# Talking-heads attention, then a SoLU MoE layer, on one core: another stored order for the attention steps

## The chip, the core and the metric

The kernel runs on one core of a Trainium2 chip. Five engines work at once, each through its own list of instructions in order: TensorE (PE, with its weight loads PEld) multiplies, VectorE (DVE) and ScalarE (ACT) do elementwise work and reductions, GpSimd (POOL) does elementwise work on SBUF and issues DMAs, SyncE (SP) issues DMAs. They wait for each other by semaphores. The metric is the time of one execution on the device in microseconds; three runs are given by their median.

## The reference

Attention with four batches, 12 heads, 448 positions and head size 64; the heads are mixed before and after the softmax. Its result is the input of a layer of 1792 tokens.

```python
scores = scale * np.matmul(q, k.transpose(0, 1, 3, 2))
scores = np.einsum('bhij,hg->bgij', scores, w_pre)
attn = np.exp(scores - np.max(scores, axis=-1, keepdims=True))
attn = attn / (np.sum(attn, axis=-1, keepdims=True) + 1e-09)
x = np.matmul(np.einsum('bhij,hg->bgij', attn, w_post), v)   # then (1792, 768)
h = x @ w_in                                                  # (1792, 1024)
solu = h * softmax(h)
out = (layer_norm(solu) * g_ln) @ w_out                       # (1792, 768)
```

## The kernel before

Matrices are split into a high and a low 16-bit part, and a product is the sum of three products of parts. The high part is a scaled copy (line 394 on ScalarE, 396 on GpSimd). The low part is what remains (line 399 on VectorE, lines 616 and 617 as two steps on GpSimd).

**Attention.** Per batch, q and k are loaded as raw_q and raw_k (line 558), their maximum is taken (588 to 590), and six pairs of heads each are split (pair_hi 607, pair_lo 613) into hl_q and hl_k. Here VectorE reads two SBUF tiles, the raw one and the high part. SP's DMA transposes (629) turn them into q and k. Rows are taken in four blocks per batch. For a block TensorE makes scores ps (735), ScalarE and VectorE split them into s (394, 758), and SP fetches s, rearranged, into sr (791): ten rows of all 12 heads are one unit, and units go in pairs. For a pair TensorE does the premix pm (822), VectorE the row maximum (834), ScalarE the exponential e with its sum sm (850). A guard adds a small number to sm (861, on GpSimd or VectorE), VectorE takes the reciprocal (865), GpSimd scales the postmix weights wq by it into wr (871), one step for each unit. TensorE then multiplies e by wr into o (881), which ScalarE or VectorE copies into p_t (403, 405). After a block TensorE multiplies by v into px (942), and xsh and xsl are split from it (394, 399). There are 92 pairs or single last units, and so 92 reciprocals; 180 units, and so 180 wr.

**w_in.** Before attention ends, w_in is loaded as 64-bit numbers in six pieces, each in four DMAs (cv_wi, line 1010), and made 32-bit numbers: on VectorE the exponent (1025), the sign (1031), the mantissa's mask (1036) and the join (1041), on ScalarE a rebias (1028), on GpSimd the product (1044). Its maximum follows (wm, 1066 or 1068), and a split into wi (394, 396, 399). The first MoE tile's matmuls (ps_h, 1111; tile 0 in 18 steps of two matmuls) are mixed into the end of attention.

**MoE.** For each of 14 tiles of 128 tokens: ps_h by TensorE (1111), then on VectorE, ScalarE and GpSimd the SoLU and the norm (u, line 1735 on), stores and transposes through memory, then the output product s (1937). w_out is converted in the same time, on VectorE above all; the matmul spread_wo (365) belongs to its scale.

**What sets the order.** Every step is a task with the engines that may do it. The class Plan once made an order by a model of costs; now two strings hold it, ORDER for attention and ORDER_MOE. A number is the place of the next task among those left, sorted by due time, and a letter (a, d, p, s) puts it on another engine than the first it names:

```python
for x in (order or self.ORDER).split():
    n = x.rstrip("adps")
    run, on = self.tasks[rest.pop(int(n))][:2]
    out.append(({"a": "act", "d": "dve", "p": "pool", "s": "sp"}[x[-1]] if n != x else next(iter(on)), run))
```

The steps are then issued in that order, so the string decides each engine's list. Semaphores are set by what a step reads, writes and takes over in buffers. No semaphore keeps steps apart that share no data.

Of the kernel before, what the change touches and what calls it, by code (L numbers as in the profile page):

```python
# [18 lines left out]
class Plan:  # L19
# [21 lines left out]
        "97 102 98 99 2604 2593 2596 95 2579 2582 99 95 2586 98 2574 99 93 2568 2596 2582 117 2568 2583 2573 101 100 "  # L41
        "119d 118 103 110a 95 103 119d 117 124 123d 130d 97d 121 88 88d 121d 92a 92a 89 88a 102 88a 88a 114 89 112 100d "
        "110 111 120 122d 89a 112 101 110 98 109a 89a 88 102 89 88d 105 88 88 94 92a 92d 101a 98 88 91 91 95a 102 154 "
        "88 106 94a 90 88 107 101a 103d 112 89 146 91 118 88 112p 90 88 147 115d 149 119 116a 121 152 110 100 109 116p "
        "119p 101 2497 124 101 137 146 2474 123 150 132 2490 2472 115d 2490 103 130 148 2492 116p 112p 135 2471 147 147 "
        "147 2469 93 102 2476 115a 116d 2480 95 2473 88 95 133 97 98 2469 123 127 126 104 125 0 103 118 97 104 2451 "
        "2449 120 124 102 97 97 97 2453 99p 2442 112 2439 100 2443 2438 87 121 96 98 87 113 98 112d 0 104 2437 97 110 "
        "2434 2424 115 116 86 94p 115 2427 93 2420 2418 95 96 2412 105 2413 122 86 104 86 112 95 99 120 112p 0 101 94 "
        "85 93 85 85 102 105 97 97 98a 85 91 109 91 97 98 91 85 89 89 89 111 2380 99 2382 0 88 2379 102 88 88a 2374 88 "
        "89 88 104 84d 87 106 87 91 84a 107 93p 91 86 87 91 86 89 98 96 93 92 87d 92 98 104 88 91 92 94 96d 90 96 101 "  # L50
        "87a 91 93 95 96 89 96 92 97 89d 92 96 85a 92 97 93 88d 94 84d 84 94 85a 91 97 91 96 0 85 87a 83 89p 89 92 94 "
        "95 94 93 85 2305 133 2302 97 84 87 86 83a 103 89 84a 93 94 86 0 92 92 120 94 96 93 2283 117 2280 84 96 84d 84 "
        "2276 2276 86 86 94 90 84a 97 84 97 90d 90 90 90 106 106 91 92 84 87 95 83a 84a 95 0 89 82 89 94 83a 92 95p 95 "
        "100 102 86 96 84 99 86a 87 82 0 83 94 80a 98 94 94 106 87 90 83 82 100 86 101 85 0 81 99 91 81a 104 98 99 98 "
        "83 92p 86 97 91 94 98 99 95 93 98 86 98 98 83 97 92 83d 84 94 85 96p 96 112 89 86 96 87 93 95 86 79 83a 91 80 "
        "0 90 82 89 85 95 93 107 124 101 83a 88 85 88 80 79d 88 82a 111 95 101 98 87 104 82 97 103 90d 83 0 79 109d 87 "
        "83 95 100 77p 81a 103 94 91 84 97 100 86 81 0 84 80a 104 87 103 103 85 93 87p 80 94 86 101 92 86 83d 86 77p 86 "
        "79 81a 95 81a 96 98 102 82 87 0 94 96 88d 100 82 81 82 96 104 82 84 0 79 82 74d 78a 94 82 81 87 81 78a 80 92 "
        "83 92 92 83 96 79 84d 96 98 96 96 84 99 89 90 74 78 77p 78d 79a 90 88 79 82 91 90 87d 80 80 89 99 91 90 0 84 "
        "89 94 79 90 111 81a 88 89 77p 88 81 73d 88p 103 79a 80 84 88 85 80 0 90 80 82 84 72 84 84 72d 87 78a 83 76 84 "  # L60
        "84 79 72 77 76a 78 82p 85 0 89 75 75 76 79 85 86 78 90 75a 72p 78 76 77 75 89 73d 81 73d 80 81d 88 74 0 75 73 "
        "86 70 72 76 95 77 76 72a 73a 72 76 94 70 0 70 80 78 88 69 69 70 69 74 75p 76 69 71 71 79 73 69 89 69d 69d 69 "
        "80 81p 78 71 87 87 77 70 69 70 70 69 74 0 80 70 73 72 83 68a 88 70 71 69d 71 80p 88 70 68 70 0 70 67 68a 83 73 "
        "73 93 76 73 79 76 67 0 72 66 75 89 66 67a 79 70 66 68 66 67 68 77 68 82 77 83 68 82 82 79 87 107 67a 76 69p 69 "
        "68d 102 66 85 87 67 88 68 73 77p 0 83 67 68 84 82 68a 73 85 81 65 70a 89 86 103 74 0 80 92 86 89 88 71 72 72 "
        "93 73 78p 117 85 89 89 74a 75a 67 111 75 82 88 91 73 74 90 74 84p 75 76 82 87 86 91 89 94 67 74 0 66 73a 82 95 "
        "88 90 75d 0 95 97 75 74 91 79 76 66 82d 95 74 88 96 75 80 90 76a 78a 71 79 84 78 99 87 103 79 0 92 96 100 78 "
        "84 104 100 85 80 101 94 74 81 97 94 85p 85 80a 103 93 81d 96 0 82 112 75d 79a 83 83 95 81 87 95 94 103 129 82 "
        "78 94 111 85p 91 85 122 92 96 60s 94 91 60p 79a 76 95 87a 100 80d 101 81 135 91d 82 60s 60p 74 95 79 86 79 88 "
        "90 76 123 90 95 60s 78a 88 0 97 79a 80 82 87 88p 73d 59s 86 75 95 85 59p 88 78 88 88 89 91 97 78 0 110 88 78 "  # L70
        "93 58p 117 77a 81 72 76a 98 112 76 58p 93 77 58s 77 70 96 88p 92 88 93 58s 58s 87 89 95 90 90 99 76a 92 94d 0 "
        "96 82a 92 97 58s 82 92 97 58s 96 82 98 82 58s 99 89 81a 85 97 94 87 87 97 58a 63 81a 85 85 58s 82 93p 0 92 80 "
        "91 92 81 84 92 94 95 84 80 91 80 96 92 64 96 87 80a 82a 89 0 97 82 55d 72 100 90p 91 90 63 98 93 80 93 81 96 "
# [2186 lines left out]
```

## Time and profile before

| | |
|---|---|
| time, median of 3 runs | 632.03 us (628.05 to 632.23) |
| the profiled execution | 632.41 us, span 630.7 us |
| PE busy | 600.8 us (95% of the span) |
| DVE busy | 551.4 us (87%) |
| ACT busy | 447.9 us (71%) |
| POOL busy | 324.1 us (51%) |
| attention's last work on TensorE | about 420 us after the start |

The profile is one execution. A share is a mean over both halves; matmuls are pipelined and their ends are modelled, so a busy TensorE isn't one at its peak. A wait is put down to the instruction whose semaphore came last.

### The profile page before, as it was taken

Reading aid. Unit: us, or ns where it says so; the run is one execution under the profiler, and the core shown is the slowest. Engines: PE = TensorE matmul, PEld = TensorE weight load, DVE = VectorE, ACT = ScalarE, POOL = GpSimd, SP = SyncE. Lnnn points to the kernel's source line nnn. Section 1 sums busy time; section 2 is a strip of 40 time slices with the busy share of each in tenths; the row PEclk is TensorE's granted clock in tenths of the full one; section 3 lists DMA queues with packets and bytes.
Section 4 is the critical chain, followed back from the end, with each engine's and each line's share of the span. In section 5 each row is a group of like instructions: output and inputs, shape, how many; then the busy total and the mean of one; then the engine's idle time right before and its main releaser. Section 6 shows DMA issues by size and latency. Waiting matters only on the chain. (4 is left out here: it accounts for less than half of the span.)

```text
span 630.7 us, 19859 instructions
## 1 busy us (share of the span) xinstructions
PE 600.8 (95%) x7650; PEld 405.1 (64%) x7650; DVE 551.4 (87%) x1301; ACT 447.9 (71%) x1003; POOL 324.1 (51%) x505
## 2 busy tenths in 40 slices
PE   7998999999999999998999998999997999999997
PEld 6665777777677777686777677764442445666664
DVE  5888999889999989996999998757999899997783
ACT  3688887889878788876899996625776987453320
POOL 2554586255793345971456436602536565475740
PEclk9999999999999999998999999999997999999999
DMA  7577478469887459799658855232584506069642
GB/s 176 157 158 224 154 160 207 152 202 207 227 203 194 169 192 200 230 188 228 230 165 202 260 196 212 113 85 81 180 221 119 162 35 164 20 151 202 157 117 75
DMA packets 134646, 106.80 MB, mean 169 GB/s; under 512 B 88388, under 2 KB 122600, under 8 KB 134552
## 3 DMA queue, kind: packets, MB, share of 16 engines
q1 hardware_dynamic: 128072, 91.43, 53.9%
q0 software_dynamic: 3904, 10.04, 6.4%
q10 hardware_dynamic: 2576, 4.06, 2.5%
q8 instruction: 60, 0.98, 0.7%
q14 instruction: 34, 0.28, 0.1%
HBM read 34.03 MB, written 16.97 MB: 81 GB/s over the span
## 5 line engine op out<-in xcount | busy, mean ns | idle before, releaser
L881 PE MATMUL o<-wr,e 128*64 128x120 f32 x2520 | 157.6, 271 | 5.1 <-POOL wr L871 3.4
L881 PEld LDWEIGHTS o<-wr,e 128*64 128x64 f32 x2520 | 134.8, 138 | 36.7 <-issue 19.3
L850 ACT ACTIVATE e<-pm,nb 128x448 f32<-128x448 f32 x180 | 114.4, 641 | 22.4 <-PE o L881 6.9
L834 DVE TENSOR_SCALAR_CACHE_REDUCE pm<-pm,c_nexp 128x448 f32<-128x448 f32 x171 | 113.7, 683 | 16.0 <-PE pm L822 13.9
L871 POOL TENSOR_SCALAR wr<-wq,sm 128x120 f32<-128x120 f32 x180 | 73.8, 418 | 89.7 <-DVE sm L865 66.1
L758 DVE SCALAR_TENSOR_TENSOR s<-ps,s 120x448 f16<-120x448 f32 (+1 forms) x180 | 105.1, 613 | 7.9 <-ACT s L394 6.9
L394 ACT ACTIVATE s<-ps 120x448 f16<-120x448 f32 (+1 forms) x180 | 90.7, 550 | 25.2 <-PE ps L735 20.6
L403 ACT COPY p_t<-o 128x480 f32<-128x480 f32 x148 | 89.1, 624 | 11.3 <-PE o L881 11.0
L942 PE MATMUL px<-p_t,raw_v 128*64 128x120 f32 (+3 forms) x1632 | 93.4, 258 | 0.9 <-DVE xsl L399 0.9
L1111 PE MATMUL ps_h<-wi,xf 128*128 128x512 f16 x396 | 88.4, 387 | 0.0
L942 PEld LDWEIGHTS px<-p_t,raw_v 128*64 128x64 f32 x1632 | 82.1, 137 | 7.2 <-issue 4.8
L735 PE MATMUL ps<-k,q 64*64 64x448 f16 (+2 forms) x972 | 76.7, 354 | 2.5 <-DVE q L399 0.8
L1111 PEld LDWEIGHTS <-xf 128*128 128x128 f16 x396 | 39.5, 100 | 48.5 <-issue 3.3
L822 PE MATMUL pm<-sr,wp_hi 64*64 64x448 f16 (+1 forms) x684 | 57.3, 358 | 7.2 <-DMA sr<-s 5.4
L861 POOL TENSOR_SCALAR sm<-sm 128x2 f32<-128x2 f32 (+1 forms) x59 | 15.0, 254 | 68.3 <-ACT e L850 62.3
L735 PEld LDWEIGHTS <-q 64*64 64x64 f16 (+1 forms) x972 | 32.5, 105 | 27.4 <-issue 14.7
L1937 PEld LDWEIGHTS <-sz 128*128 128x128 f16 x336 | 32.9, 98 | 21.7
L850 ACT ACTIVATION_READ_ACCUMULATOR e<-pm,nb 128x1 f32 x180 | 37.7, 209 | 0.0
L822 PE MATMUL pm<-sr,wp_lo 60*64 60x448 f16 (+1 forms) x342 | 36.6, 349 | 0.0
L1879 POOL TENSOR_TENSOR xs<-xs 128x512 f32<-128x512 f32 x14 | 24.1, 1720 | 22.2 <-DVE xs L1879 21.7
L1937 PEld LDWEIGHTS <-lt 128*128 128x128 f16 x252 | 24.7, 98 | 16.4
L822 PEld LDWEIGHTS <-wp_hi 64*64 64x64 f16 (+1 forms) x684 | 18.6, 105 | 25.6 <-issue 19.7
(250 smaller groups left out, 1111.1 us busy)
## 6 DMA issues: line engine op xcount, KB each, us to landing
sr<-s SPq DMA_DIRECT2D x176, 210.0 KB
cv_wi<-in_moe_w_in_dram SPq DMA_DIRECT2D x24, 256.0 KB
cv_wo<-in_moe_w_out_dram SPq DMA_DIRECT2D x8, 768.0 KB
raw_k<-in_k_dram POOLq DMA_DIRECT2D x18, 224.0 KB, 4.1
raw_q<-in_q_dram POOLq DMA_DIRECT2D x18, 224.0 KB, 7.7
ln_h<-lh SPq DMA_DIRECT2D x14, 256.0 KB
ln_l<-ll SPq DMA_DIRECT2D x14, 256.0 KB
xl<-xsl SPq DMA_DIRECT2D x9, 224.0 KB
```

The source lines that it names most:

```text
L394: nc.scalar.activation(out=hi, in_=x, func=AF.Copy, scale=s)
L403: nc.scalar.copy(out=out, in_=in_)
L735: nc.tensor.matmul(sps[b, c, h + e][lo:hi], q2[b, g][rows, 2 * j + x, i0 + lo : i0 + hi], k1[b, g][rows, 2 * j + y, 0:S], start=(a == 0), ...
L758: nc.vector.scalar_tensor_tensor(out=t[:, h, 1], in0=y, scalar=2.0**-E_S, in1=t[:, h, 0], op0=ALU.mult, op1=ALU.subtract)
L822: nc.tensor.matmul(pmx[b, u + i][64 * e : 64 * e + 64, 0:S], w[rows], sr[b, u][rows, e, z], start=(a == 0), stop=(a == 2),)
L834: nc.vector.tensor_scalar(out=pmx[b, u][:, 0:S], in0=pmx[b, u][:, 0:S], scalar1=c, scalar2=None, op0=ALU.mult, op1=ALU.min, accum_out=nb,)
L850: nc.scalar.activation(out=ee[b, u], in_=pmx.pop((b, u))[:, 0:S], func=AF.Exp, bias=nbs.pop((b, u)), scale=-1.0, accum_out=sm,)
L871: ENG[eng].tensor_scalar(out=w, in0=wq[0:UK, 0 : H * UN], scalar1=sm, scalar2=1.0, op0=ALU.mult, op1=ALU.mult)
L881: nc.tensor.matmul(o_t[g][z * JH : (z + 1) * JH, c * 120 : (c + 1) * 120], e[:, x * JH : (x + 1) * JH], w, start=True, stop=True,)
L942: nc.tensor.matmul(xps[b, blk, g][e * 64 : e * 64 + 64, i, cut], raws["v", b, g][:, 2 * i + e, c * D : (c + 1) * D], next(x for y, x in bl ...
L1111: nc.tensor.matmul(ps[:, n], xx[:, kc, o : o + 128], ww[:, kc, n * 512 : (n + 1) * 512], start=(kc == 0 and a == 0), stop=(kc == KDM - 1 a ...
L1937: nc.tensor.matmul(y, x, w, start=(n == 0), stop=(n == len(terms) - 1 ))
```

## The change

The string ORDER is another one; ORDER_MOE, all tasks, what each task does and all buffers are the same. The new order keeps VectorE's steps between SBUF tiles and all steps of GpSimd apart in its plan. The same 2627 attention tasks are issued. Some change their engine: low parts of q and k on VectorE 21 to 25 and on GpSimd 15 to 11, low parts of the first batch's k on VectorE 3 to 4 and GpSimd 3 to 2, copies of o on VectorE 32 to 35 and on ScalarE 148 to 145, maxima of w_in on VectorE 3 to none and ScalarE 3 to 6, maxima of q and v on VectorE two fewer and on ScalarE two more, five loads of v from SP to GpSimd, and one guard, one score copy and one copy of q.

```diff
     ORDER = (
-        "97 102 98 99 2604 2593 2596 95 2579 2582 99 95 2586 98 2574 99 93 2568 2596 2582 117 2568 2583 2573 101 100 "
...
+        "97 96 101 102 97 2593 98 99 100 119 103 2588 2597 2582 2571 95 93 119 119d 100 103 95 119 120d 126 133d 125a "
...
     )
```

Two places of the new lists follow. The names end in a running number that differs between the kernels; the one ahead of it counts batch and unit, as in sm_3_28 (batch 3, unit 28).

**VectorE and GpSimd late in batch 3**, where pieces 4 and 5 of w_in are converted. VectorE before:

```order
L1025 TENSOR_SCALAR cv_wi5_6911<-cv_wi5_6911 128x1024
L399 SCALAR_TENSOR_TENSOR xsl3_7005<-px_3_0_1_7065,x_sc_77,xsh3_7004 128x120 x3
L834 TENSOR_SCALAR pm_3_30_7123,nb_3_30_7162<-pm_3_30_7123,c_nexp_75 128x448
L834 TENSOR_SCALAR pm_3_31_7124,nb_3_31_7164<-pm_3_31_7124,c_nexp_75 128x448
L758 SCALAR_TENSOR_TENSOR s_3_3_6770<-ps_3_3_10_7111,s_3_3_6770 90x448
L758 SCALAR_TENSOR_TENSOR s_3_3_6770<-ps_3_3_11_7112,s_3_3_6770 90x448
L865 RECIPROCAL sm_3_28_7119<-sm_3_28_7119 128x2
L834 TENSOR_SCALAR pm_3_32_7190,nb_3_32_7214<-pm_3_32_7190,c_nexp_75 128x448
L1031 SCALAR_TENSOR_TENSOR cv_wi5_6911<-cv_wi5_6911 128x1024
L834 TENSOR_SCALAR pm_3_33_7191,nb_3_33_7233<-pm_3_33_7191,c_nexp_75 128x448
L1036 TENSOR_SCALAR cv_wi5_6911<-cv_wi5_6911 128x1024
L865 RECIPROCAL sm_3_30_7185<-sm_3_30_7185 128x2
```

VectorE now:

```order
L1025 TENSOR_SCALAR cv_wi5_6950<-cv_wi5_6950 128x1024
L399 SCALAR_TENSOR_TENSOR xsl3_7037<-px_3_0_1_7060,x_sc_77,xsh3_7036 128x120 x3
L834 TENSOR_SCALAR pm_3_30_7132,nb_3_30_7153<-pm_3_30_7132,c_nexp_75 128x448
L758 SCALAR_TENSOR_TENSOR s_3_3_6761<-ps_3_3_10_7116,s_3_3_6761 90x448
L834 TENSOR_SCALAR pm_3_31_7133,nb_3_31_7160<-pm_3_31_7133,c_nexp_75 128x448
L1031 SCALAR_TENSOR_TENSOR cv_wi5_6950<-cv_wi5_6950 128x1024
L865 RECIPROCAL sm_3_28_7095<-sm_3_28_7095 128x2
L758 SCALAR_TENSOR_TENSOR s_3_3_6761<-ps_3_3_11_7117,s_3_3_6761 90x448
L865 RECIPROCAL sm_3_30_7157<-sm_3_30_7157 128x2
L1036 TENSOR_SCALAR cv_wi5_6950<-cv_wi5_6950 128x1024
L834 TENSOR_SCALAR pm_3_32_7209,nb_3_32_7241<-pm_3_32_7209,c_nexp_75 128x448
L399 SCALAR_TENSOR_TENSOR xsl3_7037<-px_3_1_0_7171,x_sc_77,xsh3_7036 128x120 x3
```

The mask step of piece 5 (1036) stood ahead of the reciprocal of unit 30, behind a row maximum; it now stands behind that reciprocal, which now comes ahead of the row maxima of units 32 and 33. GpSimd there, before:

```order
L871 TENSOR_SCALAR wr_3_27_7151<-wq_74,sm_3_26_7037 128x120
L861 TENSOR_SCALAR sm_3_28_7119<-sm_3_28_7119 128x2
L871 TENSOR_SCALAR wr_3_28_7220<-wq_74,sm_3_28_7119 128x120
L871 TENSOR_SCALAR wr_3_29_7229<-wq_74,sm_3_28_7119 128x120
L861 TENSOR_SCALAR sm_3_30_7185<-sm_3_30_7185 128x2
L1044 TENSOR_TENSOR wi3_6598<-cv_wi4_6636 128x1024
L871 TENSOR_SCALAR wr_3_30_7258<-wq_74,sm_3_30_7185 128x120
```

GpSimd now:

```order
L871 TENSOR_SCALAR wr_3_27_7101<-wq_74,sm_3_26_7031 128x120
L871 TENSOR_SCALAR wr_3_26_7125<-wq_74,sm_3_26_7031 128x120
L1044 TENSOR_TENSOR wi3_6418<-cv_wi4_6758 128x1024
L861 TENSOR_SCALAR sm_3_28_7095<-sm_3_28_7095 128x2
L861 TENSOR_SCALAR sm_3_30_7157<-sm_3_30_7157 128x2
L871 TENSOR_SCALAR wr_3_28_7188<-wq_74,sm_3_28_7095 128x120
L871 TENSOR_SCALAR wr_3_29_7231<-wq_74,sm_3_28_7095 128x120
```

The product of piece 4 (1044) stood behind the guards (861) of units 28 and 30 and behind wr of unit 28; it now stands ahead of both guards and of that wr.

**SP late in batch 2**, where the last transposes of batch 3's q and k (629), fetches of score rows (791) and the first loads of w_in (1010) meet. Before:

```order
L629 DMA_TRANSPOSE k_3_2_5394<-hl_k3_4831 128x16x112
L791 DMA sr0_132<-s_2_3_4828 120x1x896 x2
L791 DMA sr1_133<-s_2_3_4828 120x1x896
L629 DMA_TRANSPOSE q_3_2_5513<-hl_q3_4883 128x16x112
L791 DMA sr1_133<-s_2_3_4828 120x1x896
L1010 DMA cv_wi0_5606<-in_moe_w_in_dram 128x512
L791 DMA sr2_134<-s_2_3_4828 120x1x896
L1010 DMA cv_wi0_5606<-in_moe_w_in_dram 128x512
L791 DMA sr2_134<-s_2_3_4828 120x1x896
```

Now:

```order
L791 DMA sr0_132<-s_2_3_4830 120x1x896 x2
L791 DMA sr1_133<-s_2_3_4830 120x1x896
L629 DMA_TRANSPOSE k_3_2_5476<-hl_k3_4771 128x16x112
L791 DMA sr1_133<-s_2_3_4830 120x1x896
L629 DMA_TRANSPOSE q_3_2_5497<-hl_q3_4773 128x16x112
L791 DMA sr2_134<-s_2_3_4830 120x1x896
L1010 DMA cv_wi0_5505<-in_moe_w_in_dram 128x512
L791 DMA sr2_134<-s_2_3_4830 120x1x896
L791 DMA sr3_135<-s_2_3_4830 120x1x896
```

The transpose of k stood ahead of both fetches into sr0 and the first into sr1, and now stands behind them; the second fetch into sr1 stood behind the transpose of q, and now stands ahead of it. One load of w_in instead of two stands ahead of the second fetch into sr2.

At the head, GpSimd's loads of w_pre and w_post (470) stand ahead of the steps that make the identity, and 2 instead of 20 warm-up matmuls (704) ahead of the first transposes of k on TensorE (647). At the tail, 9 instead of 4 of the 18 steps of MoE's first tile (1111) stand behind the last px.

## Rows read from the trace of the kernel before

**Rows 1.** Stretches: length, busy of PE, PEld, DVE, ACT, POOL; clock, DMA share, GB/s:
```profile
25.00:420.00 395.00, 377.86 (x6348) 283.39 (x6342) 355.54 (x960) 320.38 (x775) 215.52 (x416) 1.00 0.70 190
```

**Rows 2.** Timeline at the seam (start, length, what, idle before), then the chain's end:
```profile
437.20 1.28 DVE L1735 TENSOR_SCALAR_CACHE_REDUCE u<-ps_h,ch 128x1024 f32<-128x1024 f32 x1 [3.16 <-PE ps_h L1111]
...
480.62 0.77 PE L365 MATMUL spread_wo<-ident,amx_wo 128*128 128x128 f32 x2 [4.61 <-DVE sm L1757]
...
481.39 49.17 PE ps_h L1111 x216
```

**Rows 3.** TensorE's waits, 0 to 400 us (total, times, longest):
```profile
PE pm L822 <- DMA sr<-s: 5.4, 4, 2.6
PE o L881 <- POOL wr L871: 3.4, 5, 1.7
...
PE ps L735 <- DMA q<-hl_q: 0.6, 1, 0.6
```

**Rows 4.** Timeline of 380 to 384 us:
```profile
379.64 2.42 POOL L1044 TENSOR_TENSOR wi<-cv_wi 128x1024 f32<-128x1024 f32 x1
...
380.00 2.61 DVE L1036 TENSOR_SCALAR cv_wi<-cv_wi 128x1024 uint32<-128x1024 uint32 x1
...
382.85 0.36 POOL L871 TENSOR_SCALAR wr<-wq,sm 128x120 f32<-128x120 f32 x1 [0.80 <-DVE sm L865]
383.27 0.93 PE L881 MATMUL o<-wr,e 128*64 128x120 f32 x13 [1.69 <-POOL wr L871]
```

**Rows 5.** VectorE's groups in attention (busy us, mean ns), then two undisturbed instances:
```profile
L399 DVE SCALAR_TENSOR_TENSOR hl_k<-raw_k,p_kq,hl_k 112x256 f16<-112x256 f32 x24 | 15.4, 684 | 0.0
...
L399 DVE SCALAR_TENSOR_TENSOR hl_q<-raw_q,p_kq,hl_q 112x256 f16<-112x256 f32 x18 | 8.9, 539 | 0.0
...
L1036 DVE TENSOR_SCALAR cv_wi<-cv_wi 128x1024 uint32<-128x1024 uint32 x6 | 6.1, 1019 | 0.0
...
86.41 0.85 DVE L399 SCALAR_TENSOR_TENSOR hl_k<-raw_k,p_kq,hl_k 112x256 f16<-112x256 f32 x2
...
368.84 0.67 DVE L1036 TENSOR_SCALAR cv_wi<-cv_wi 128x1024 uint32<-128x1024 uint32 x1
```

**Rows 6.** GpSimd's wr as a group, then wr alone in two stretches:
```profile
L871 POOL TENSOR_SCALAR wr<-wq,sm 128x120 f32<-128x120 f32 x180 | 73.8, 418 | 89.7 <-DVE sm L865 66.1 <-PE o L881 4.0 <-ACT e L850 3.9
...
110.00:160.00 50.00, 8.91 (x26) 1.00 0.68 189
...
300.00:400.00 100.00, 22.29 (x48) 1.00 0.69 216
```

**Rows 7.** Two further groups of VectorE in attention:
```profile
L405 DVE COPY p_t<-o 128x480 f32<-128x480 f32 x32 | 20.6, 647 | 1.6 <-PE o L881 1.3 <-PE px L942 0.3
...
L1068 DVE TENSOR_REDUCE am_wi<-wi 128x1 f32<-128x1024 f32 x3 | 3.6, 1208 | 0.0
```

**Rows 8.** Timeline of SP and TensorE, 284 to 298 us, and that stretch's clock:
```profile
284.16 2.55 SPq L791 DMA_DIRECT2D sr<-s  x3
286.81 1.76 SPq L629 DMA_TRANSPOSE q<-hl_q  x1
288.67 1.35 SPq L791 DMA_DIRECT2D sr<-s  x1
...
288.69 1.66 PE L881 MATMUL o<-wr,e 128*64 128x120 f32 x28
...
294.03 0.57 PE L822 MATMUL pm<-sr,wp_hi 64*64 64x448 f16 x7 [2.56 <-DMA sr<-s]
...
295.29 3.07 PE L881 MATMUL o<-wr,e 128*64 128x120 f32 x28
...
280.00:300.00 20.00, 17.39 (x272) 13.25 (x273) 14.17 (x41) 13.53 (x35) 4.57 (x14) 0.91 0.93 224
```

**Rows 9.** Timeline of the head, and the chain's steps of the first MoE tile:
```profile
5.79 1.76 PE L647 MATMUL pt_k<-ident,raw_k 112*64 112x112 f32 x16 [2.06 <-DMA raw_k<-in_k_dram]
...
413.08 3.56 PE ps_h L1111 x16
```

152 rows, old and new, of the table ORDER are left out of this document.

## The prediction

> **What bounds the kernel now.** I read the stretches first, then the chain of waits at the seam between the two halves, then the waits of TensorE, and last the groups of VectorE and GpSimd. Attention fills the span up to about 420 us. From 25 to 420 us TensorE is busy 377.9 of 395 us, VectorE 355.5, ScalarE 320.4 and GpSimd 215.5 [rows 1]. So TensorE sets the pace and has 17.1 us without work in that stretch; VectorE is close behind it with 39.5 us.
>
> What the end of the kernel hangs on is read at the seam. VectorE runs out of work at 434 us and waits 3.16 us for the matmuls of the third MoE tile. From there a chain of its work leads to a matmul for which TensorE waits 4.61 us, and from 481 us on TensorE's own matmuls lead on to the end [rows 2]. MoE is unchanged, so the end moves by just what TensorE gains or loses before those matmuls: a microsecond of TensorE's waits in attention is a microsecond of the kernel, and no other engine's time counts by itself.
>
> Two kinds of those waits can be named: 5.4 us in four waits for score rows fetched by DMA, and 3.4 us in five waits for wr, the small weight that GpSimd makes for each unit's postmix [rows 3].
>
> **What the change may remove.** The clearest case is at 380 us. GpSimd starts the product of a w_in piece (2.42 us). VectorE starts a tensor_scalar between SBUF tiles 0.36 us later and needs 2.61 us for what takes 0.67 us alone; the reciprocal behind it comes late, so does wr, and TensorE stands for 1.69 us [rows 4]. The stretching is general. Of the low parts of q and k, a pair of instructions alone takes 0.85 us; 12 pairs for k cost 15.4 us and 9 for q 8.9 us, so 5.2 and 1.3 us too much; the six mask steps of line 1036 cost 6.1 us for 6 times 0.67, or 2.1 too much [rows 5]. That is 8.6 us of VectorE. On GpSimd wr takes 0.34 us in a stretch without such VectorE steps (8.91 us for 26), 0.46 us where w_in is converted (22.29 for 48), and all 180 cost 73.8 us, some 12 us too much [rows 6].
>
> The Trainium skill (page "SBUF — State Buffer", section "Who interferes with whom") says that VectorE's second pair of SBUF ports is GpSimd's, and that whichever engine starts first holds it for its whole instruction while the other stands still. The 380 us case agrees: VectorE's step ends 0.55 us after GpSimd's product does.
>
> How far apart the new order keeps them can be counted. A wr starts when the reciprocal on VectorE is done. Of VectorE's steps between SBUF tiles (low parts of line 399 read from SBUF, and lines 1025 to 1041), 20 stand first or second behind one of the 92 reciprocals in the order of before, and 12 in the new one. At the 380 us place, the product of piece 4 now stands ahead of two guards (sm, line 861) on GpSimd, and VectorE's mask step behind the two reciprocals that wait for these guards: it can't start before the product is done. That is a new wait as well: behind these reciprocals queue a score's low part, the mask step and a row maximum, for which ScalarE's exponentials wait, and up to the product's 2.4 us can be lost there if it starts late.
>
> **Sum, term by term.** (1) wr: TensorE's 3.4 us; nothing to all of it. I take 2.0, since 12 of 20 close neighbours stay, but the longest wait, 1.69 us, is one that the order takes apart. (2) VectorE: about half of 8.6 us, 4.3 us, is freed. Work also moves. Four low parts come over from GpSimd (4 times 0.85, +3.4 us) and three copies of o from ScalarE (3 times 0.65, +1.9), and three maxima of w_in go to ScalarE (3 times 1.21, -3.6) [rows 5, 7]. Six more swaps (two maxima, a split, a score copy, a q copy, a guard) are single steps of both signs, taken as nothing. So VectorE's work falls by 4.3 - 1.7 = 2.6 us. Of this TensorE sees between nothing and all; I take 1.5, since both engines are nearly full and hold each other by the score banks. ScalarE's additions lie in its 75 us of free time, as do five loads of v that move from SP's queue to GpSimd's in GpSimd's 179 us [rows 1]; without that cover each costs its issue.
>
> (3) SP's queue before 294 us. TensorE stands 2.56 us for the second half of an sr pair, fetched at 288.67, behind the transpose of q issued at 286.81. This stop costs a second time: the window's granted clock is 0.91, and the 28 postmix matmuls behind it take 3.07 us instead of 1.66, so 1.4 us [rows 8]. In the new order that fetch stands ahead of the transpose of q but behind that of k, which itself comes three fetches later. If the wait goes, 4.0 us are won; if the k transpose is late in its place, nothing. I take half, 2.0.
>
> (4) The head. GpSimd now issues three loads before it makes the identity, and 2 instead of 20 warm-up matmuls stand before the first transposes. These wait 2.06 us, until 5.79 us, for the load of k in any case [rows 9]: nothing. Without that cover it would be up to those 2.06 us.
>
> (5) The tail. Nine instead of four steps of MoE's first tile (two matmuls each, 0.45 us by 16 in 3.56 us [rows 9]) stand behind the last attention matmuls. This lets attention end about 2.2 us earlier against TensorE's work, and MoE's VectorE work start earlier; but at 434 us VectorE waits 3.16 us for TensorE anyway and would then wait 5.4 [rows 2]. Nothing.
>
> Together 2.0 + 1.5 + 2.0 = 5.5 us. The profiled execution took 632.4 us (span 630.7 and 1.7 around it), which is 0.4 above the median of 632.03: 632.4 - 5.5 = **626.9 us**.
>
> **Bounds.** If all idle time of TensorE between 25 and 420 us went, with the 1.4 us of low clock, it would be 632.4 - 18.5 = 613.9 us; no way down goes further. If nothing reaches TensorE it is 632.4.
>
> **Rivals.**
> *The waits only change their name.* Steps kept apart still take their turns: while one engine holds off, the other waits as it would have been held. For it speaks that TensorE's large stops (294 us, and the waits for fetched rows) are not where the stretched steps are, and that GpSimd's 180 idle us show that its lateness mostly costs nothing. Against it speaks 380 us, where the order of the rows decides. Then terms 1 and 2 are nothing: 632.4 - 2.0 = 630.4 us, or 632 without the third. The Trainium skill's rule on the ports speaks for this rival: by it an order wins only where other work fills the time that the one step would have been held.
>
> *VectorE was the true bound.* Row maxima and low score parts come early everywhere and most of TensorE's 17.1 us close. For it: VectorE is 90% busy [rows 1]. Against: 5.4 us of TensorE's waits are for DMAs [rows 3], which this doesn't touch. Three quarters of 18.5 us would give 618.5 us.
>
> *Transposes come late (slower).* The transposes of k and q for the next batch need all low parts, and the last of these moved: at batch 3 the k transpose stands three fetches further back, about 2.5 us at 0.85 us for an issue [rows 8], and in batch 1 the last high parts stand later on GpSimd. The first score matmuls of a batch come right behind; TensorE already waits for such a transpose once, for 0.6 us [rows 3], so there is no lead to use up. At 2.6 us in each of three batches, with the clock's 1.4 us each as at 294 us, it is 12.0 us, less 1.5 for term 1: 632.4 + 10.5 = 642.9 us. It decides from about 2 us a batch. Against it: in the counted order the last transposes and first scores of each batch stand within one premix pair of where they were.
>
> *It doesn't do what it says.* The order holds only rows on each engine, and no wait keeps the engines apart, so a microsecond of drift brings the steps together again; that ends at 630 to 634 us, with the first rival.
>
> **How the numbers follow.** My forecast, 3 to 9 us off: 45%. Nothing reaches TensorE: 22%. VectorE was the bound, 614 to 622: 13%. Slower: 20%, of which a quarter is small. The range takes the forecast and the first rival whole, most of the third and the small part of the slower one: 616 to 639 us; the forecast's own range is 623 to 630. One per cent is about what a measurement can tell from no change, 6.3 us: 625.7 and 638.4. Of the forecast's 45 some 20 lie below 625.7, with the 13 that makes 0.33. The slower rival puts 0.16 above 638.4. The rest, 0.51, is within.
>
> **What would show it.** Right: pairs of low parts (hl_k, hl_q) near 0.85 us, no mask step over 1 us, wr near 0.36 us in the w_in stretch, no stop for wr over 1 us, and VectorE still waiting for the third tile with the wait grown to some 5 us. Wrong: waits of score matmuls for transposes above 1 us at the three batch starts, or new stops for fetched rows; a low granted clock in another window; VectorE no longer waiting at the third tile, by which term 5 would count; or VectorE idle before reciprocals that wait for GpSimd.

## The result, and the profile after

The new order is slower: **638.2 us** (median of 4 runs, 636.82 to 640.64) against 631.7 (median of 4, 628.05 to 632.23), a ratio of 1.012 with a 95% interval of 1.007 to 1.0169. Ratios leave out executions more than 1.5% above the fastest of the same kernel; where that changes a reading, the medians of all runs stand beside them. The profiled execution took 636.82 us with a span of 635.1, so it stands 4.4 us above the one of before, where the medians differ by 6.5.

The stretch of [rows 1], after:

```profile
25.00:420.00 395.00, 376.44 (x6274) 281.26 (x6272) 352.88 (x967) 320.43 (x778) 203.68 (x404) 0.99 0.71 190
```

TensorE is busy 1.5 us less than before (376.4 for 377.9), at a granted clock of 0.99. VectorE is less busy by 2.7 us here and GpSimd by 11.8, but as after falls behind, the same window holds less of the program: over the whole execution the pages have VectorE at 549.8 us for 551.4 and GpSimd at 311.6 for 324.1. How far after falls behind: the same step of MoE's first tiles (ps_h) starts at 426.14 us instead of 421.46.

What stands around the end (timeline of after, then a step of its chain), which answers [rows 2]:

```profile
441.88 1.28 DVE L1735 TENSOR_SCALAR_CACHE_REDUCE u<-ps_h,ch 128x1024 f32<-128x1024 f32 x1 [3.17 <-PE ps_h L1111]
...
485.32 0.77 PE L365 MATMUL spread_wo<-ident,amx_wo 128*128 128x128 f32 x2 [4.63 <-DVE sm L1757]
```

```profile
486.09 49.07 PE ps_h L1111 x216
```

Every row there is 4.7 us later than in [rows 2] and the waits are the same (3.17 for 3.16, 4.63 for 4.61). The end moved by what TensorE lost in attention, as the prediction had it; only the sign differs.

TensorE's waits of after, 0 to 400 us (total, times, longest), to be laid beside [rows 3]:

```profile
PE pm L822 <- DMA sr<-s: 3.6, 5, 1.2
PE ps L735 <- DVE s L758: 3.6, 8, 2.2
PE o L881 <- ACT p_t L403: 2.6, 5, 1.0
PE ps L735 <- DMA q<-hl_q: 2.3, 2, 1.7
...
PE spread_kq L365 <- DVE amx_kq L387: 1.7, 1, 1.7
...
PE o L881 <- POOL wr L871: 0.7, 1, 0.7
```

And those of before that grew, in the same view:

```profile
PE spread_kq L365 <- DVE amx_kq L387: 1.0, 2, 0.7
...
PE o L881 <- ACT p_t L403: 0.9, 3, 0.5
...
PE ps L735 <- DVE s L758: 0.5, 3, 0.2
```

Waits for wr fell from 3.4 to 0.7 us and for score rows from 5.4 to 3.6. In their place stand waits for a score bank (0.5 to 3.6), for copies of o (0.9 to 2.6), for transposes (0.6 to 2.3) and for the maximum of k and q (1.0 to 1.7). Without the two rows of the start (the warm-up's and that of the first transposes, which begin at 5.71 us for 5.79), the list's sum goes from about 15.9 to 17.4 us, a third of what this execution lost. The rest is the clock: behind three of the new stops it was granted at half speed, the level of 1.2 GHz instead of 2.4. Its mark is the length of 28 postmix matmuls: 1.66 us at full clock, as in [rows 8], and 2.4 to 3.1 with half speed among them. In before one such place stands ahead of 400 us, that of [rows 8]; in after there are three, at 50, 166 and 252 us, and none at 294. At a granted clock of 0.91 over 20 us, one of them costs 0.09 x 20 = 1.8 us, so two more are some 3.5 us. With 1.5 us of waits that is about the 4.7.

### The profile page after: what moved, and what is told of

Same layout as the page of the kernel before. It is cut to its first block, busy times and chain, and to the rows that moved or that the text cites. A ratio compares the mean times of both kernels' runs of the same rounds, so it can differ in the third digit from the quotient of the medians.

```text
span 635.1 us, 19843 instructions
## 1 busy us (share of the span) xinstructions
PE 601.8 (95%) x7650; PEld 403.9 (64%) x7650; DVE 549.8 (87%) x1307; ACT 449.3 (71%) x1010; POOL 311.6 (49%) x493
## 4 chain that ended last, share of the span: by engine, by line
PE 60%; DVE 17%; DMA 13%; issue 4%; ACT 3%; POOL 2%; SPq 0%; DVEq 0%; ACTq 0%; POOLq 0%
PE s L1937 15%; PE o L881 13%; PE ps_h L1111 9%; PE px L942 8%; PE ps L735 6%; PE pm L822 5%; DMA sr<-s 5%; DMA raw_v<-in_v_dram 4%; DVE s L758 3%; DVE pm L834 3%; DMA q<-hl_q 2%; DVE ll L1686 2%; DMA raw_q<-in_q_dram 1%; DVE hl_k L399 1%; PE warm L704 1%
## 5 line engine op out<-in xcount | busy, mean ns | idle before, releaser
L871 POOL TENSOR_SCALAR wr<-wq,sm 128x120 f32<-128x120 f32 x180 | 69.7, 396 | 115.0 <-DVE sm L865 66.6
L403 ACT COPY p_t<-o 128x480 f32<-128x480 f32 x145 | 87.7, 624 | 5.5 <-PE o L881 4.7
L735 PE MATMUL ps<-k,q 64*64 64x448 f16 (+2 forms) x972 | 78.3, 360 | 6.1 <-DVE s L758 3.6
L735 PEld LDWEIGHTS <-q 64*64 64x64 f16 (+1 forms) x972 | 33.5, 106 | 30.5 <-issue 15.9
L822 PE MATMUL pm<-sr,wp_lo 64*64 64x448 f16 (+1 forms) x342 | 37.3, 355 | 0.0
```

Of the source, the lines that this page charges most:

```text
L403: nc.scalar.copy(out=out, in_=in_)
L735: nc.tensor.matmul(sps[b, c, h + e][lo:hi], q2[b, g][rows, 2 * j + x, i0 + lo : i0 + hi], k1[b, g][rows, 2 * j + y, 0:S], start=(a == 0), ...
L822: nc.tensor.matmul(pmx[b, u + i][64 * e : 64 * e + 64, 0:S], w[rows], sr[b, u][rows, e, z], start=(a == 0), stop=(a == 2),)
L871: ENG[eng].tensor_scalar(out=w, in0=wq[0:UK, 0 : H * UN], scalar1=sm, scalar2=1.0, op0=ALU.mult, op1=ALU.mult)
```

## Experiments

The letters: A is the list of tasks in the order of after, B that of before. `up_to(X, t)` is the tasks that X issues until TensorE is at t us in the profile of before; a composed order takes the tasks of its parts one after the other and leaves out what is issued already. Ratios are to the kernel before, with their 95% intervals; a granted clock is the mean over a kernel's runs, beside that of the runs of before made with them. In 632 us, 0.001 of that clock is 0.63 us.

### Where in the program the time is lost

**Last third in the new order, and first part in it.**

```diff
-tasks = B
+tasks = up_to(B, 296) + A      # l1
+tasks = up_to(A, 187) + B      # l2
```

> The order of before up to the first scores of batch 3 (about 296 us), then the rest of the tasks in the order of after. Theory 'the loss sits in the batch joints 1 to 3, not in the conversion of w_in': on TensorE's list after is 5.0 us behind at 301 us and 4.7 us at the end, so this piece is worth about -0.3 us: 631 to 632 us, as before. Rival 'the separated steps pay where w_in is converted' (term 1 of the forecast): the waits for wr of 3.4 us shrink to 0.7, about 629 us. Rival 'the separation itself costs everywhere': 633 to 634 us.

> The order of after up to the end of batch 1 (about 200 us), then the rest in the order of before. By the traces after is 3.5 us behind at 200 us, of which two half-speed stretches of the clock (at 50 and 166 us) are 3.4: 635 us if those come again, about 632 us if they are chance.

l1: 0.9988 [0.9958, 1.0019]. l2: 1.0097 [1.0062, 1.0133]. The stretch in which w_in is converted, with the 380 us case of [rows 4], is worth between 2.7 us gained and 1.2 us lost: neither a loss to speak of, nor all of the 3.5 us of terms 1 and 2, part of which would lie earlier. Most of the loss lies before 187 us.

**VectorE's and GpSimd's lists alone**, on the lists of before of the other engines.

```diff
-lists = {PE: B, ACT: B, SP: B, DVE: B, POOL: B}
+lists = {PE: B, ACT: B, SP: B, DVE: A, POOL: A}
```

> VectorE's and GpSimd's lists (and the engines of the steps) as in after, the lists of TensorE, ScalarE and SP as in before. Theory 'DMA traffic is bunched by the new order of SP and of the loads': the loads of k and q and part of those of v stand on GpSimd, so part of the loss comes with it: 633 to 636 us. Rival 'the separation of the steps costs by itself' (a step held back is a step late): all of it, 638 us. If VectorE's and GpSimd's lists bring what was forecast and the loss is in the other lists: 627 to 630 us.

1.1646 [1.1601, 1.169], 735.4 us. This says nothing on whether keeping the steps apart costs by itself: lists of two plans wait for each other everywhere, for instance px for its split 13.4 us and o for wr 11.9 us in its profile. What it does show is the price of lists that don't fit, 104 us.

**The loads of v back** on the queues and places of before (13 of GpSimd's rows and 12 of SP's move).

```diff
-v loads: as in A
+v loads: engine and place as in B, all else as in A
```

> The order of after, with the 48 loads of v for batches 1 to 3 on the queue and behind the TensorE step where before has them; nothing else moved (13 rows on GpSimd, 12 on SP). Theory 'the late fetches at the joints come from where the loads of v stand': the stops at 165 us (2.3 us), 235 to 240 us (1.6) and the half-speed stretch at 166 us (1.7) go, about 632.5 us. Rival 'the loads of v only happen to be in flight there': unchanged, 638 us.

1.0092 [1.006, 1.0123]: most of the loss stays, and in its profile TensorE stops for 3.6 us at 166 us, with half speed behind. The queues and places of these loads are not its main cause.

**Three pieces of the first part.**

```diff
-tasks = B
+tasks = up_to(A, 63) + B                     # s1
+tasks = up_to(B, 63) + up_to(A, 117) + B     # s2
+tasks = up_to(B, 117) + up_to(A, 187) + B    # s3
```

> The order of after up to premix pair 19 of batch 0 (about 63 us), the rest in the order of before. By the milestones of TensorE after is 1.0 to 1.4 us ahead at 77 us, half-speed stretch at 50 us included: 629.5 us, 1 us below before. If that stretch is no chance and the gain ahead of it is: 632.

> The order of before with only the stretch from premix pair 19 of batch 0 to the scores of batch 1's second block (63 to 117 us) in the order of after. Theory 'transposes of q come late at the start of batch 1' (the stop of 1.8 us at 111 us): +2 us, 632.5 us. Rival 'the same stop of up to 2.1 us is in the order of before too' (103.6 us in the trace of l1_last_third): no change, 630.5 us.

> The order of before with only the stretch from 117 to 187 us in the order of after. Theory 'the loss is the stop at 165 us and the half-speed stretch behind it': TensorE stands 2.3 to 3.6 us there instead of 1.2 to 1.5, and a stretch of 3.4 us at half speed costs 1.7 more: +3 to +4 us, 634 us, most of the whole loss. Rival 'the loss is spread over the whole first part': +2 us, 632.5 us.

s1: 1.0056 [1.0019, 1.0093], clock 0.9899 beside 0.9944. s2: 1.0008 [0.9972, 1.0044]. s3: 1.0066 [1.0024, 1.0108], clock 0.9930. The medians of all runs are 632.76, 629.86 and 633.61 us beside 630.97, so s1 and s3 stand 1.8 and 2.6 us above before where the ratios say 3.5 and 4.2. The head and the stretch from 117 to 187 us carry the loss. In the head most of it or all is clock: 0.0045 is 2.8 us. In the other stretch little is: 0.0014 is 0.9 us, and s3's profile has no half speed there.

**Both of these back in the order of before**, the rest as in after.

```diff
-tasks = A
+tasks = up_to(B, 63) + up_to(A, 117) + up_to(B, 187) + A
```

> The order of after with the stretches to 63 us and from 117 to 187 us in the order of before. If these two carry the whole loss (each alone cost 0.6% on before): 630 to 632 us, as before, ratio 0.998 to 1.002. If the middle stretch from 187 to 296 us costs as well (a stop of 1.7 us and a half-speed stretch at 252 us in the profile of after): 634 us.

1.0023 [0.9995, 1.0052], 634.14 us: of 1.2% about 0.2% is left, and that can't be told from nothing.

### The head: a stop that costs its clock

TensorE in after, 46 to 58 us:

```profile
46.69 1.03 PE L881 MATMUL o<-wr,e 128*64 128x120 f32 x14
...
48.49 0.35 PE L822 MATMUL pm<-sr,wp_hi 64*64 64x448 f16 x1 [0.76 <-DMA sr<-s]
50.04 0.57 PE L822 MATMUL pm<-sr,wp_hi 64*64 64x448 f16 x7 [1.21 <-DMA sr<-s]
...
52.40 2.42 PE L881 MATMUL o<-wr,e 128*64 128x120 f32 x28
...
57.40 0.84 PE L704 MATMUL warm<-ident 128*128 128x128 f16 x12
```

The granted clock from 50 to 54 us (columns of [rows 1]):

```profile
50.00:54.00 4.00, 3.96 (x41) 2.39 (x42) 3.08 (x8) 1.50 (x4) 0.22 (x1) 0.58 0.77 236
```

Before, the waits for the same kind of fetches:

```profile
54.31 0.57 PE L822 MATMUL pm<-sr,wp_hi 64*64 64x448 f16 x7 [1.39 <-DMA sr<-s]
...
59.19 0.57 PE L822 MATMUL pm<-sr,wp_hi 64*64 64x448 f16 x7 [0.85 <-DMA sr<-s]
...
63.15 0.57 PE L822 MATMUL pm<-sr,wp_hi 64*64 64x448 f16 x7 [0.63 <-DMA sr<-s]
```

Before waits more in all (2.9 us in three places, 4 to 5 us apart). After waits 2.0 us, but in one place with a single matmul between, and the 28 matmuls behind it take 2.42 us. To see whether it is the clock, I gave TensorE matmuls on the identity in that place.

```diff
-def warm(e):
+def warm(e, n=2):
...
-    for i in range(2):
+    for i in range(n):
...
-    warm,
+    lambda e, i=i: warm(e, 6 if i in (0, 2, 25, 29, 35, 42, 47) else 2),
...
-tasks = up_to(A, 63) + B
+tasks = up_to(A, 63) + B, these 7 warm tasks ahead of the premix at 48 us
```

> The kernel s1 (order of after to 63 us, then of before) with 42 warm-up matmuls of TensorE, 28 of them additional, right ahead of the premix that waits for late fetches at 49 to 51 us: the wait is as long as before, but TensorE works through most of it. Theory 'the loss of s1 is the half-speed stretch that follows the stop': the mean granted clock of its runs rises from 0.990 to 0.994, as in before, and the time falls by 1.7 us to 631. Rival 'the stop itself is the loss': 632.8 us or a little more, whatever the clock.

0.999 [0.9963, 1.0017], clock 0.9938 beside 0.9929. The loss of s1 is gone. Of the 42 matmuls without use, 28 are new; the other 14 stood behind the stop (in after 12 at 57.40 us, and 2 at 50.81), so up to 1.2 us of the gain is their move into the wait. The profile of w1:

```profile
47.88 2.52 PE L704 MATMUL warm<-ident 128*128 128x128 f16 x42
50.32 0.75 PE L822 MATMUL pm<-sr,wp_hi 64*64 64x448 f16 x8
...
51.77 1.66 PE L881 MATMUL o<-wr,e 128*64 128x120 f32 x28
```

The premix comes no earlier for it (50.32 for 48.49 and 50.04), but the postmix behind it runs at full clock. Half speed at this place stands in 4 of 6 profiles with the head of after, in none of 9 with that of before and none of 4 with the filled one. The two stops come to 2.0 to 2.6 us in all six, so their length doesn't tell which execution falls. s1's own profile is one of the two without half speed; and as one such stretch costs about 1.7 us (0.42 of 4 us), it can't be all of the 2.8 us of clock that the runs of s1 lose.

**The same in the order of before**, at the longest wait of all, the 4.61 us of [rows 2]; then with the filled head as well.

```diff
 ps.append(bank(f"spread_{name}"))
+for _ in range({"wo": 76}.get(name, 0)):
+    nc.tensor.matmul(ps[0][:, 0:128], ident, ident, start=True, stop=True)
```

> The kernel before, with 76 additional matmuls on the identity in the bank of spread_wo, right ahead of the matmul for which TensorE waits 4.6 us at 476 to 481 us. The wait stays, but TensorE works through it; the 6.8 us at half speed that follow it cost 3.4 us. Theory 'the low clock follows the idle stretch, and what it costs is added to the wait': 628 us, 3.4 below before, mean granted clock 0.997 to 0.999. Rival 'the half-speed stretches come anyway, or cost nothing on the path': 631 to 632 us.

> The kernel w1 (order of after to 63 us with its stop filled, then the order of before) and the same fill ahead of spread_wo: w1's 631 less 3.4 = 627.5 us, below both kernels of the case. Rival as for k1: 631 us.

k1: 0.9971 [0.9943, 1.0000], clock 0.9975 beside 0.9935. k2: 0.9994 [0.9963, 1.0025], clock 0.9971.

```profile
479.41 4.41 PE L365 MATMUL spread_wo<-ident 128*128 128x128 f16 x76
```

The clock gains 0.004, or 2.5 us, and the time falls by 0.3%: k1 has the lowest ratio of all, but its interval reaches 1. k2, with the head of after, adds nothing to it. The clock is clearer than the time: half speed follows this wait (2.9 to 4.6 us long) in 17 of the 18 profiles without the fill, and in neither of the two with it.

**Two stops of after filled**, the head's and the one at 252 us, whose rows are (TensorE, then VectorE, of after):

```profile
249.33 0.95 DVE L590 TENSOR_REDUCE am_kq<-raw_q 112x1 f32<-112x768 f32 x1 [1.13 <-DMA raw_q<-in_q_dram]
...
251.77 1.04 PE L365 MATMUL spread_kq<-ident,amx_kq 128*128 128x128 f32 x4 [1.68 <-DVE amx_kq L387]
```

Loads of raw_q come late for the maximum, and TensorE's spread of that maximum stands for it. The edit is that of w1 in A and the fill above with `{"kq3": 24}`; k4 has the lists of p2, below, too.

```diff
-for _ in range({"wo": 76}.get(name, 0)):
+for _ in range({"kq3": 24}.get(name, 0)):
```

> The order of after, with the stop at 49 us filled as in w1 and the stop at 252 us filled with 24 matmuls on the identity ahead of spread_kq of batch 3. Theory 'half of what after loses is low clock behind its stops': two of its three half-speed stretches in attention go, 638 - 3.4 = 634.6 us, mean granted clock from 0.988 to 0.993. Rival 'the stops themselves are the loss': 637 to 638 us.

> As k3, and the three lists at 165 us mended as in p2. If stop and clock at these three places are all that after loses: 631 to 633 us, as before. If the rest of the new order costs too: 635 us.

k3: 1.0095 [1.0056, 1.0134], clock 0.9909. k4: 1.0089 [1.0056, 1.0122], clock 0.9908. Against 1.012 and 0.988 the clock is better by 0.003, some 2 us, and the time by as much within its interval. At 252 us the fill was too short in k3's profile (lines moved by two):

```profile
247.50 1.51 PE L365 MATMUL spread_kq<-ident 128*128 128x128 f16 x24
251.01 0.71 PE L367 MATMUL spread_kq<-ident,amx_kq 128*128 128x128 f32 x4 [1.99 <-DVE amx_kq L389]
```

In k4's profile the same fill covers the wait: that spread starts at 250.64 us without one, and the granted clock from 246 to 258 us is 1.00, where k3 has 0.86. The time of k4, which differs from k3 by the lists alone, can't be told from that of k3.

### The stretch around 165 us

Here the last block of a batch gets its scores. s has two buffers that take turns, so ScalarE's first split of that block (line 394) waits until the last fetch of an earlier block has read the buffer. The trace names a load of v as the releaser; the split reads no v, and by the buffers it is the fetch, issued by 151 us and landed at 163.24, 0.3 us before the split starts. The DMA queues of after, 148 to 166 us, show what is under way in the meantime (packets, MB, share of 16 engines):

```profile
q1 hardware_dynamic: 4174, 2.33, 62.8%
q0 software_dynamic: 532, 1.15, 27.4%
```

The 16 engines are 90% busy, by the issues in that stretch mostly with fetches and loads of v. That this is why the fetch takes 12 us fits, but no run shows it. What stands behind that split in after (ScalarE, VectorE, TensorE):

```profile
163.57 0.97 ACT L394 ACTIVATE s<-ps 90x448 f16<-90x448 f32 x2 [2.48 <-DMA raw_v<-in_v_dram]
...
164.15 1.15 DVE L758 SCALAR_TENSOR_TENSOR s<-ps,s 90x448 f16<-90x448 f32 x2 [2.09 <-ACT s L394]
...
164.82 0.35 PE L735 MATMUL ps<-k,q 64*90 64x448 f16 x1 [2.23 <-DVE s L758]
...
165.22 0.68 DVE L834 TENSOR_SCALAR_CACHE_REDUCE pm<-pm,c_nexp 128x448 f32<-128x448 f32 x1
...
166.01 2.49 PE L881 MATMUL o<-wr,e 128*64 128x120 f32 x28
```

And before:

```profile
162.23 0.97 ACT L394 ACTIVATE s<-ps 90x448 f16<-90x448 f32 x2 [1.08 <-DMA raw_v<-in_v_dram]
...
163.86 0.56 PE L822 MATMUL pm<-sr,wp_hi 60*64 60x448 f16 x6 [0.94 <-ACT e L850]
```

The lists at this place (o16 is the postmix of unit 16, m22 the premix of 22; copy, exp and max belong to units too; split, low and scores to the last block):

```
             before                                          after
TensorE      o16 o17 m22 scores2 o18                         o16 scores2 o17 o18 m22
ScalarE      copy14 exp18 exp19 max_v copy15 split0 split1   copy14 split0 split1 copy15 max_v
             exp20                                           copy16 exp20
VectorE      max20 max21 low1 low0                           low0 low1 max20 max21
```

In after the steps that hang on the fetch stand ahead of steps that are ready, on all three engines at once: the split ahead of the copies of o, its low part ahead of two row maxima, the second scores ahead of two postmix steps. So all three stop for the same DMA, for 2.48, 2.09 and 2.23 us, and the clock falls behind it.

**One step back, on TensorE alone**: the second scores behind o17, o18 and m22.

```diff
-o16 scores2 o17 o18 m22 scores4
+o16 o17 o18 m22 scores2 scores4
```

> The order of after with one step of TensorE moved: the second pair of score matmuls of the last block of batch 1 stands behind the postmix of units 17 and 18 and the premix of units 22 and 23, as in before, instead of ahead of them. Theory 'TensorE is held at 165 us by scores that stand ahead of work that is ready, while their buffer waits for a late fetch': the stop shrinks by the two postmix steps of about 1 us each that can now run, and the half-speed stretch behind it goes: 638 - 2 - 1.7 = 634.5 us. Rival 'that work is not ready either' (the premix waits for the same fetch, wr for GpSimd): 637 to 638 us.

1.0143 [1.0068, 1.0219], clock 0.9843. The theory that one place of TensorE's list does it fell. The stop only moved to a postmix step that waits for a copy of o, which stands behind ScalarE's split:

```profile
164.12 0.97 ACT L394 ACTIVATE s<-ps 90x448 f16<-90x448 f32 x2 [3.70 <-DMA raw_v<-in_v_dram]
...
165.73 3.15 PE L881 MATMUL o<-wr,e 128*64 128x120 f32 x28 [3.85 <-ACT p_t L403]
```

**All three lists mended.**

```diff
-TensorE o16 scores2 o17 o18 m22 scores4
+TensorE o16 o17 o18 m22 scores2 scores4
-ScalarE copy14 split0 split1 copy15 max_v copy16 exp20
+ScalarE copy14 copy15 copy16 exp20 split0 split1 max_v
-VectorE low0 low1 max20 max21
+VectorE max20 max21 low0 low1
```

> The order of after with the joint at 165 us mended on three lists: on ScalarE the first two splits of the last block's scores (which wait for the late fetch) stand behind two copies of o and one exponential, on VectorE behind two row maxima, and on TensorE the second pair of scores behind two postmix steps and a premix (one step moved on TensorE, three on ScalarE, two on VectorE). Theory 'steps that wait for the late fetch stand ahead of ready work on all three lists': the stop at 165 us falls from 2.3 to 4 us to about 1.2, as in before, and the half-speed stretch behind it goes: 638 - 3 to 4 = 634.5 us. Rival 'the late fetch holds the rest anyway': 637 to 638 us.

1.0077 [1.0041, 1.0114], clock 0.9868, against 1.012 [1.007, 1.0169] of after: the intervals overlap. In its profile the stop at 165 us is gone, but another stands 4 us behind it, with half speed after that one:

```profile
166.10 1.01 PE L881 MATMUL o<-wr,e 128*64 128x120 f32 x14 [0.18 <-ACT p_t L403]
...
170.08 0.35 PE L735 MATMUL ps<-k,q 64*90 64x448 f16 x1 [1.14 <-DVE s L758]
```

**The same place in the order of before**: only 153 to 167 us of after; only what lies around it; and the first with its three lists mended as in p2.

```diff
-tasks = B
+tasks = up_to(B, 153) + up_to(A, 167) + B                                      # j1
+tasks = up_to(B, 117) + up_to(A, 153) + up_to(B, 167) + up_to(A, 187) + B      # j2
+tasks = j1 with TensorE o16 o17 o18 m22 scores2, ScalarE and VectorE as in p2  # j3
```

> The order of before with only the stretch from premix pair 16 to the postmix of unit 22 of batch 1 (about 153 to 167 us) in the order of after. Theory 'the loss of the piece from 117 to 187 us is the joint': a stop of about 2 us at 162 to 165 us with a half-speed stretch behind it in the profile, 634 us, ratio 1.004 to 1.007. Rival 'it is spread over the piece': 1.000 to 1.002.

> The complement: the order of before with the stretches 117 to 153 us and 167 to 187 us in the order of after, the joint between them as in before. Theory of the joint: as before, 0.999 to 1.001, and no half-speed stretch at 165 us. Rival 'spread': 1.003 to 1.005.

> j1 with its lists mended as in p2, and on TensorE also the third pair of scores behind the first two px of the batch (two steps moved on TensorE, three on ScalarE, two on VectorE; the fetches and loads stay as in after). If the place of the waiting steps on the lists is the cause: ratio 1.000 to 1.002. If the fetches and loads of after are: as j1.

j1: 1.0042 [1.0011, 1.0074], clock 0.9894 beside 0.9938. j2: 1.0037 [1.0004, 1.0070], clock 0.9922. j3: 1.0033 [0.9996, 1.0070], clock 0.9928. Those 14 us suffice for a loss, and in j1 it is the same stop, grown:

```profile
163.18 0.97 ACT L394 ACTIVATE s<-ps 90x448 f16<-90x448 f32 x2 [4.43 <-DMA raw_v<-in_v_dram]
...
164.42 1.81 PE L735 MATMUL ps<-k,q 64*90 64x448 f16 x6 [3.90 <-DVE s L758]
```

But j2 loses as much without them. In its profile TensorE stops there too, for a copy of o:

```profile
163.93 1.39 PE L881 MATMUL o<-wr,e 128*64 128x120 f32 x14 [2.77 <-ACT p_t L403]
```

The stretch 160 to 180 us (columns of [rows 1]) in before, after, j1 and j3:

```profile
160.00:180.00 20.00, 18.59 (x282) 12.95 (x280) 18.81 (x58) 16.91 (x42) 17.35 (x33) 1.00 0.87 214
```

```profile
160.00:180.00 20.00, 17.59 (x237) 12.05 (x238) 17.29 (x54) 15.48 (x39) 11.92 (x23) 0.91 0.91 226
```

```profile
160.00:180.00 20.00, 16.09 (x211) 11.41 (x207) 14.76 (x42) 14.49 (x36) 11.09 (x19) 0.83 0.92 229
```

```profile
160.00:180.00 20.00, 18.25 (x251) 12.55 (x248) 17.99 (x55) 16.74 (x42) 13.42 (x24) 1.00 0.96 236
```

Mending the lists gives the clock back (0.83 to 1.00 in the profile, 0.9894 to 0.9928 over the runs) and TensorE 2.2 us of work in those 20. The time, 1.0042 to 1.0033, can't be told apart. All profiles together say the same of the stop: with the lists of after at this place TensorE's longest stop is 1.6 to 3.9 us and half speed follows in 6 of 7 (p1 among them; all but s3); with the three lists mended the stops are at most 1.3 us, yet half speed is still there in 2 of 3 (p2 and k4, some 4 us later); with the order of before the longest is 0.9 to 2.8 us, with half speed in 2 of 9 (j2 and k2). So the order on the three lists causes the long stop, and makes half speed likelier. That it is the whole loss between 117 and 187 us isn't shown; j2, and s3 with its clock of 0.9930, speak against it, and no pair of runs (after and p2, k3 and k4, j1 and j3) shows that mending it saves time.

## Why the prediction was wrong

**What held.** The seam: a microsecond of TensorE ahead of it was a microsecond of the kernel, and the tail was worth nothing, though VectorE's wait for the third tile stayed at 3.17 us and did not grow to 5.4. Term 1: the waits for wr fell by 2.7 us where I took 2.0, and are 0.7 to 1.1 us in all six profiles with the whole list of after (with the loads of v moved, stops filled or lists mended among them), against 2.9 to 4.4 in the eleven that end in that of before.

**Term 2's freed time held at one step only.** Groups of VectorE and GpSimd after, beside [rows 5] and [rows 6]:

```profile
L871 POOL TENSOR_SCALAR wr<-wq,sm 128x120 f32<-128x120 f32 x180 | 69.7, 396 | 115.0 <-DVE sm L865 66.6 <-ACT e L850 14.8 <-PE o L881 7.5
...
L399 DVE SCALAR_TENSOR_TENSOR hl_q<-raw_q,p_kq,hl_q 112x256 f16<-112x256 f32 x28 | 14.6, 562 | 0.0
L399 DVE SCALAR_TENSOR_TENSOR hl_k<-raw_k,p_kq,hl_k 112x256 f16<-112x256 f32 x22 | 13.4, 651 | 0.0
...
L1036 DVE TENSOR_SCALAR cv_wi<-cv_wi 128x1024 uint32<-128x1024 uint32 x6 | 4.3, 712 | 0.0
```

The six mask steps are nearly as short as one alone (712 ns for 0.67 us). But before, only one of the six was stretched, the 2.61 us of [rows 4]; their median was 0.69. "The stretching is general" was read from a mean. The low parts are hardly shorter: 651 for 684 ns for k, 562 for 539 for q, so a pair is still far from 0.85 us, and wr, 69.7 us for 73.8 in all, takes 0.44 us where w_in is converted, not 0.36. By the prediction's own count VectorE's excess went from 8.6 to 7.0 us: 1.6 us were freed, not 4.3. VectorE's busy time over the whole execution fell by 1.6 us where the sum had 2.6; with 1.6 freed and 1.7 moved in it would not have fallen, so that nearness is luck. The 380 us case of [rows 4] went as read from the order (after; GpSimd, then VectorE):

```profile
376.88 2.58 POOL L871 TENSOR_SCALAR wr<-wq,sm 128x120 f32<-128x120 f32 x2 [1.15 <-DVE sm L865]
...
379.43 2.86 POOL L1044 TENSOR_TENSOR wi<-cv_wi 128x1024 f32<-128x1024 f32 x1
...
384.42 0.67 DVE L1036 TENSOR_SCALAR cv_wi<-cv_wi 128x1024 uint32<-128x1024 uint32 x1
```

The mask step is clear of the product and takes 0.67 us for 2.61. Two wr at 376.88 now take 2.58 us instead, beside a join of VectorE (1041) at 377.68: "a microsecond of drift brings the steps together again" held as well.

**Term 3** came true at its place: the stop of 2.56 us became two of 0.59 and 0.78, 3 us apart, with no half speed behind them:

```profile
300.10 0.76 PE L735 MATMUL ps<-k,q 64*64 64x448 f16 x12 [0.59 <-DMA q<-hl_q]
...
303.53 0.57 PE L822 MATMUL pm<-sr,wp_hi 64*64 64x448 f16 x7 [0.78 <-DMA sr<-s]
```

It is no chance of one execution: between 285 and 310 us half speed stands in none of the 7 profiles with the order of after there, and in 7 of the 12 with that of before.

**The step of term 2 that failed**: "of this TensorE sees between nothing and all; I take 1.5". No run shows that it saw any of it: l1, the part in which the one long stretching went, is 0.9988, which allows a gain of 2.7 us at most for terms 1 and 2 together. What could be seen was 1.6 us, not 4.3.

**The step of the sum that failed**: its terms are all waits taken away. The order moved rows on every engine, and what the moved rows would wait for in their new places was priced at nothing. For that there was no reason: "single steps of both signs" speaks of six swaps of engine, and the new wait that the prediction did see, up to 2.4 us behind the product of piece 4, is not in the sum either. The runs show some 6.5 us more instead of 5.5 less: about 3.5 of it is clock (0.9880 over the runs of after for some 0.9935 of before, times 632). The other 3 are what is left, new stops beyond those taken away; in the one profile the list of waits grew by 1.5. The places are the head and the stretch from 117 to 187 us: with both of them as in before, 1.0023 is left of 1.012.

**The clock was priced at one place only.** [rows 8] had its price, 1.4 us behind one stop, and I counted it as a gain of term 3 and as a loss in the slower rival alone. s1 and w1 show what that left out: with two waits in the head that are shorter in all than before's, but close together, the clock of the runs is 0.9899 and the ratio 1.0056; with matmuls without use in them it is 0.9938 and 0.999. I had costed the head at nothing by its warm-up matmuls and first load. That held, as the first transposes start no later, but I read no further than 6 us; the stop is at 48 to 50.

**The slower rival had the wrong place.** Its total, 642.9, was nearer than the forecast, by luck. Waits for transposes did grow (0.6 to 2.3 us in the list), but the longer of the two, 1.69 us at 111 us, lies in the piece of s2, which costs nothing, and in profiles that have the order of before at that place the same stop is anything from 0.5 to 2.1 us. Its counterargument, "the last transposes and first scores of each batch stand within one premix pair of where they were", is where the reading stopped: at 165 us one premix pair was enough, for the last block's scores, since what moved ahead of ready work on all three lists was what waits for a fetch.

**What stays open.** Whether the loss between 117 and 187 us comes from the three lists at 165 us or from the transfers that arrive there late in any case: j1 and j2 lose the same, and mending (p2, k4, j3) is not told apart in time. The 0.2% of c2 has no place; nor is the fill at 252 us settled, which covered the wait in one of two profiles.

## What to carry to other kernels

A reordering is not the sum of the waits that it removes: go through each engine's new list for steps that wait for a DMA and now stand ahead of ready ones, and look at the lists that feed them too, since mending one list only moved the stop (p1). Where TensorE is full, price every new stop twice, once for the wait and once for the clock behind it, and look whether short stops now stand close together; where a stop can't be taken away, matmuls on the identity in it cost no time that could be measured and can keep the clock (w1, k1). Don't count freed time of an engine as a gain before you have seen the one that sets the pace wait for it (l1), and read the median and the longest instance of a group before you multiply its mean by its count.

## What the runs showed of the hardware

Two stops with one matmul between them (0.76 and 1.21 us in after, 2.0 to 2.6 us together) took TensorE to half speed in 4 of 6 profiles, while separate stops of up to 1.8 us at about the same place (1.39, 0.85 and 0.63 us in before, 4 to 5 us apart) did in none of 9. A wait of 2.9 to 4.6 us ahead of one spread of a maximum was followed by half speed in 17 of 18 profiles, and in neither of two with matmuls on the identity in it. One fetch of score rows, issued while the 16 DMA engines were 90% busy, landed some 12 us after its issue; putting the loads of v back on the queues of before changed nothing that can be told from after (d1).
